# Softmax exponentials by quarter of the tokens, for all heads at once, with the maximum subtracted on VectorE first

## The chip, the cores and the metric

The kernel runs on one core of one Trainium2 chip. The metric is the device time of one execution in microseconds (us); lower is better. The granted clock is the share of TensorE's full clock that the chip allows it. Runs of a state called slow (a longer time at a lower granted clock) are left out of every ratio. The profile is one execution taken by the hardware profiler; its span runs from the first to the last instruction and is about 1.3 us shorter than the device time.

## The reference

One token for each of two batch entries goes through an adaLN-conditioned block: grouped-query attention over a cached context, then an MLP.

```python
B, Sq, D = (2, 1, 1024); Hq, Hkv, Sk, Dh = (32, 4, 32768, 128)   # B part: F = 3584
mod = (_silu(c) @ w_mod).reshape(c.shape[0], 6, 1, -1)
h = _layernorm(x) * (1 + ca) + sa
# attention, q from h @ wq; each K/V head serves 8 query heads
scores = jnp.einsum('bhqd,bhkd->bhqk', q, k) * Dh ** (-0.5)
p = _softmax(scores, axis=-1)
o = jnp.einsum('bhqk,bhkd->bhqd', p, v)
x = x + ga * (o @ wo)
h = _layernorm(x) * (1 + cb) + sb
x = x + gb * (_gelu(_layernorm(h) @ w1 + b1) @ w2 + b2)
```

All inputs are bf16. K and V together are 134.2 MB, the weights about 44 MB. Each byte is used once, so there is little arithmetic for each byte fetched.

## The kernel before

The eight pairs of batch entry and K/V head are eight rounds of a loop. A round fetches two halves of K (4 MB each) and one V (8 MB), each into one buffer that is reused in the next round. The sync engine issues the transfers in this order, and each waits until the previous user of its place is done:

```python
def add_k(i, hf):   # 2 x 16 KB in each partition
    add(("K", i, hf), [2, TPC * D], ..., hf * 32 * KB, f"K{hf}")
def add_v(i):       # NCH = 4 quarters x 16 KB in each partition
    add(("V", i), [NCH, TPC * D], ..., 64 * KB, "V")
...
for i in range(NBG):
    add_k(i, 0); add_k(i, 1); add_v(i)
# then wo, w1, w2 into the places that K, V and wq leave
```

In a round TensorE transposes K in groups of 8 tiles (`tr`), ScalarE and VectorE evict the transposes, and TensorE makes the scores from them (`qk`). Then come the softmax over 8 heads and the product with V (`pv`):

```python
def softmax_3():    # the maximum of each head, times -SCALE, on all partitions
    pe(... psM[:, 128:128 + HPG] ...)
    dve(lambda e: e.tensor_scalar(negm[:, :], psM[:, 128:128 + HPG], -SCALE, None, ALU.mult), ...)
def exp(h):         # one head, all 256 columns, row sum accumulated
    act(lambda e: e.activation(E_sb[:, :, h, :], S_sb[:, h, :]..., ACT.Exp, bias=negm[:, h:h + 1], scale=SCALE,
                               accum_out=rowsum[:, h:h + 1]), reads=ROW + ["negm"], writes=["E_sb", "rowsum"], ...)
def pv(i, cc):      # a quarter of the tokens: 16 matmuls with 512 columns
    ... reads=[it.reg, "E_sb"], writes=["psO"] ...
def row_sums():     # rowsum -> rsum16 (VectorE) -> sum over partitions (TensorE) -> reciprocal
    ...
for i in range(NBG):
    ...             # transposes and scores
    softmax_1(); softmax_2(); softmax_3()
    for h in range(HPG):
        exp(h)
    row_sums()
    for cc in range(NCH):
        pv(i, cc)
    extract(); extract_2(i)
```

An exponential of one head covers the tokens of all four quarters, so the first quarter of `pv` needs all eight of them. The program also puts the matmul of `row_sums` ahead of `pv`.

## Time and profile before

| what | before |
|---|---|
| device time, median | 420.11 us (3 runs, 420.03 to 420.19) |
| bytes read from HBM | 178.28 MB |
| busy: TensorE, VectorE, ScalarE | 281.7, 169.6, 167.9 us of 418.9 |
| end of the loop of eight rounds | 374.05 us |

These lines are from the page of the profile of the kernel before: the span, the busy tenths of the DMA engines in 40 equal slices, the bytes per second in those slices, the bytes in all, and the shares of the chain of work that ended last.

```profile
span 418.9 us, 11665 instructions
...
DMA  9989999999999999999999999999999999999995
GB/s 373 449 380 449 444 408 487 397 410 442 447 432 422 435 444 426 429 447 451 404 429 469 419 413 441 447 432 422 447 432 422 419 460 451 389 441 433 417 435 243
...
HBM read 178.28 MB, written 0.00 MB: 426 GB/s over the span
...
PE 56%; DMA 22%; ACT 8%; issue 7%; DVE 6%; SPq 0%; ACTq 0%
```

The DMA line shows 9, that is 90% or more, in every slice but the third, an 8, and the last, a 5. The last line gives 56% of the chain to TensorE. The chain follows what ran without a visible wait.

The view by windows: each line is one round, cut where its last matmul ends. After the window come its length, then busy us (and instructions) of PE, PEld, DVE, ACT and POOL, the granted TensorE clock, the share of the DMA engines' time and GB/s.

```profile
core 0: us, PE busy (x) PEld busy (x) DVE busy (x) ACT busy (x) POOL busy (x), PEclk, DMA share, GB/s
62.50:106.86 44.36, 32.89 (x585) 27.72 (x585) 18.70 (x34) 20.44 (x33) 0.00 (x0) 0.76 1.01 432
145.03:182.99 37.96, 28.32 (x585) 24.27 (x586) 19.16 (x36) 20.01 (x33) 0.44 (x2) 0.87 1.01 436
297.73:336.02 38.29, 28.65 (x585) 24.27 (x586) 19.16 (x36) 20.01 (x33) 0.44 (x2) 0.87 1.00 431
```

A round moves 16.78 MB, which takes 38.7 us at 433 GB/s. TensorE's rounds 2 to 8 take 37.7 to 39.3 us. The DMA engines have no idle time in any of them (share 1.00 or 1.01). What TensorE waits for in the whole kernel is in the view of the waits. A line names the engine, what it was about to write and the line of the kernel, then what it waited for; the numbers are us in total, times, longest:

```profile
PE psM L584 <- DVE rsum L583: 45.3, 8, 5.7
...
PE psM L596 <- DVE msum L591: 13.0, 8, 1.6
...
PE psKT L534 <- DMA K<-in_A_k_cache_dram: 4.6, 1, 4.6
```

It waits for the row sums ahead of PV in each round, for the sums of the masked output behind PV, and for a K transfer only once, in round 1. In the other rounds K has landed before it is wanted. The timeline of round 7 shows the first of these waits from inside (start, duration, engine, line, operation; in brackets the idle time just before):

```profile
321.97 0.17 DVE L563 TENSOR_SCALAR negm<-psM 128x8 f32<-128x8 f32 x1 [0.48 <-PE psM L562]
322.25 0.51 ACT L566 ACTIVATE E_sb<-S_sb,negm 128x256 bf16<-128x256 f32 x1 [2.71 <-DVE negm L563]
...
326.68 0.51 ACT L566 ACTIVATE E_sb<-S_sb,negm 128x256 bf16<-128x256 f32 x1
327.09 0.19 ACT L566 ACTIVATION_READ_ACCUMULATOR E_sb<-S_sb,negm 128x1 f32 x1
...
327.31 0.23 DVE L583 COPY rsum<-rowsum 128x128 f32<-128x128 f32 x1 [5.18 <-ACT E_sb L566]
...
327.59 0.59 PE L584 MATMUL psM<-onesf,rsum 128*128 128x1 f32 x2 [5.67 <-DVE rsum L583]
...
328.11 5.80 PE L576 MATMUL psZ<-V,E_sb 128*32 128x512 bf16 x64
```

Each exponential comes with a read of its accumulator (0.19 us), and the eight follow each other every 0.63 us. The maximum is ready at 322.14 us and the first PV matmul starts at 328.11. In those 6.0 us TensorE does one small matmul. This gap is what the change aims at.

### The profile page before, as it was taken

The page shows a single profiled execution, that of the slowest core. Times are in us where ns is not written, and L with a number is a line of the kernel's source. Part 1 is how long each engine was busy: PE and PEld are TensorE (multiplying, and loading weights), DVE is VectorE, ACT ScalarE, POOL GpSimd, SP SyncE. Part 2 cuts the span into 40 slices and gives each one's busy share as a digit, 9 for nine tenths or more (in the row PEclk, how much of TensorE's full clock was granted, in tenths as well). Part 3 has the DMA queues.
Part 4 walks back from the last instruction along what each step waited for, and adds up shares of the span by engine and source line. Part 5 has one row for each costly group of instructions (what it writes and reads, how often), then busy time and mean ns, then how long its engine had stood idle before and what let it go on. Part 6 is the DMA issues. An engine that isn't in the chain of part 4 may idle for free.

```text
span 418.9 us, 11665 instructions
## 1 busy us (share of the span) xinstructions
PE 281.7 (67%) x5183; PEld 223.5 (53%) x5183; DVE 169.6 (40%) x351; ACT 167.9 (40%) x275; POOL 6.8 (2%) x29
## 2 busy tenths in 40 slices
PE   1407539856892798389559928974895699274456
PEld 1104219852892498169529915972694299132314
DVE  1201106540772377157417724760574177220421
ACT  2000015544565166526545662645265356600100
POOL 3000000000000000000000000000000000000000
PEclk9976668965997799599869968995998699686565
DMA  9989999999999999999999999999999999999995
GB/s 373 449 380 449 444 408 487 397 410 442 447 432 422 435 444 426 429 447 451 404 429 469 419 413 441 447 432 422 447 432 422 419 460 451 389 441 433 417 435 243
DMA packets 5582, 178.43 MB, mean 426 GB/s; under 512 B 698, under 2 KB 706, under 8 KB 964
## 3 DMA queue, kind: packets, MB, share of 16 engines
q1 hardware_dynamic: 5572, 178.28, 98.7%
q8 instruction: 8, 0.13, 0.1%
q14 instruction: 2, 0.02, 0.0%
HBM read 178.28 MB, written 0.00 MB: 426 GB/s over the span
## 4 chain that ended last, share of the span: by engine, by line
PE 56%; DMA 22%; ACT 8%; issue 7%; DVE 6%; SPq 0%; ACTq 0%
PE psKT L534 28%; PE psZ L576 11%; DMA K<-in_A_k_cache_dram 10%; DMA w<-in_B_w_dram 9%; PE psS L546 6%; PE psZ L546 5%; ACT E_sb L566 4%; DMA wmod<-in_w_mod_dram 4%; DVE msum L591 2%; ACT KT_sb L538 2%; DVE m1c L551 1%; ACT S_sb L550 1%; PE psM L584 1%; PE psM L562 1%; PE psM L596 1%
## 5 line engine op out<-in xcount | busy, mean ns | idle before, releaser
L534 PE MATMUL psKT<-ident,K 128*128 128x128 bf16 x2048 | 154.5, 221 | 4.6 <-DMA K<-in_A_k_cache_dram 4.6
L538 ACT ACTIVATE KT_sb<-psKT 128x1024 bf16<-128x1024 bf16 x96 | 97.7, 1025 | 115.6 <-PE psKT L534 115.4
L540 DVE COPY KT_sb<-psKT 128x1024 bf16<-128x1024 bf16 x160 | 106.3, 689 | 44.3 <-PE psKT L534 43.5
L534 PEld LDWEIGHTS psKT<-ident,K 128*128 128x128 bf16 x2048 | 118.7, 98 | 5.8 <-DMA K<-in_A_k_cache_dram 4.7
L546 PE MATMUL psS<-qcur,KT_sb 128*128 128x8 bf16 x1024 | 44.3, 166 | 1.7 <-issue 1.7
L576 PE MATMUL psZ<-V,E_sb 128*32 128x512 bf16 x512 | 44.8, 527 | 0.0
L546 PE MATMUL psZ<-qcur,KT_sb 128*128 128x8 bf16 x1024 | 43.1, 167 | 0.8
L566 ACT ACTIVATE E_sb<-S_sb,negm 128x256 bf16<-128x256 f32 x64 | 32.5, 508 | 25.1 <-DVE negm L563 23.3
L546 PEld LDWEIGHTS psS<-qcur,KT_sb 128*128 128x128 bf16 x1024 | 39.2, 96 | 1.8 <-issue 1.8
L546 PEld LDWEIGHTS psZ<-qcur,KT_sb 128*128 128x128 bf16 x1024 | 37.9, 96 | 2.0 <-ACT KT_sb L538 1.4
L584 PE MATMUL psM<-onesf,rsum 128*128 128x1 f32 x16 | 4.7, 362 | 45.3 <-DVE rsum L583 45.3
L576 PEld LDWEIGHTS psZ<-V,E_sb 128*32 128x32 bf16 x512 | 16.7, 127 | 24.2 <-issue 20.0
L584 PEld LDWEIGHTS psM<-onesf,rsum 128*128 128x128 f32 x16 | 4.0, 311 | 46.1 <-DVE rsum L583 46.1
L589 DVE TENSOR_SCALAR msum<-psZ,mk 128x128 f32<-128x128 f32 x8 | 2.8, 351 | 43.1 <-PE psZ L576 43.1
L583 DVE COPY rsum<-rowsum 128x128 f32<-128x128 f32 x8 | 1.8, 227 | 41.4 <-ACT E_sb L566 41.4
L467 PE MATMUL psS<-wmod,inT 128*32 128x512 bf16 x32 | 4.8, 592 | 16.4 <-DMA wmod<-in_w_mod_dram 16.4
L551 DVE TENSOR_REDUCE m1c<-psZ 128x8 f32<-128x512 f32 x16 | 11.1, 693 | 10.2 <-ACT S_sb L550 10.1
L596 PE MATMUL psM<-msum,hmat 128*128 128x128 f32 x16 | 3.9, 326 | 13.0 <-DVE msum L591 13.0
L551 DVE TENSOR_REDUCE m1c<-psS 128x8 f32<-128x512 f32 x16 | 11.1, 693 | 3.2 <-ACT S_sb L550 3.1
L434 ACT ACTIVATE stat<-stat 128x2 f32<-128x2 f32 x3 | 0.6, 203 | 29.4 <-DVE stat L433 29.4
L557 PE MATMUL psM<-identf,m 128*8 128x128 f32 x16 | 3.4, 298 | 13.1 <-DVE m L554 13.1
L550 ACT ACTIVATE S_sb<-psZ 128x512 f32<-128x512 f32 x16 | 9.5, 595 | 6.1 <-PE psZ L546 6.1
(121 smaller groups left out, 172.7 us busy)
## 6 DMA issues: line engine op xcount, KB each, us to landing
K<-in_A_k_cache_dram SPq DMA_DIRECT2D x16, 4096.0 KB, 25.2
wq<-in_A_wq_dram SPq DMA_DIRECT2D x2, 4096.0 KB, 44.9
wo<-in_A_wo_dram SPq DMA_DIRECT2D x2, 4096.0 KB, 36.3
w<-in_B_w_dram SPq DMA_DIRECT2D x2, 3584.0 KB, 30.6
wmod<-in_w_mod_dram SPq DMA_DIRECT2D x1, 6144.0 KB, 30.0
w<-in_B_w_dram SPq DMA_DIRECT2D x3, 2048.0 KB, 35.7
wmod<-in_w_mod_dram SPq DMA_DIRECT2D x1, 4608.0 KB, 15.9
wmod<-in_w_mod_dram SPq DMA_DIRECT2D x1, 1536.0 KB, 6.2
```

What stands on the lines that cost most here:

```text
L467: pe(lambda e, w=it.view, k=k, kk=kk, ch=ch, n=n, q=q: e.matmul(bank[n][32 * q:32 * q + 32, :], lhsT=inT[:, k, :], rhs=w[:, kk, ch * 512:( ...
L534: pe(lambda e, kq=kq, jj=jj, w=kt, t=t: e.transpose(psKT[kq][:, jj * 128:(jj + 1) * 128], w[:, t, :], ident[:, :]), reads=[it.reg, "ident" ...
L538: act(lambda e, src=src: e.activation(KT_sb[g8][:, :, :], src, ACT.Copy), reads=[f"psKT{kq}"], writes=[f"KT_sb{g8}"], sem=f"ev{cc}_{g8}")
L540: dve(lambda e, src=src: e.tensor_copy(KT_sb[g8][:, :, :], src), reads=[f"psKT{kq}"], writes=[f"KT_sb{g8}"], sem=f"ev{cc}_{g8}")
L546: pe(lambda e, t=t, jj=jj: e.matmul(ps[:, t * HPG:(t + 1) * HPG], lhsT=KT_sb[g8][:, jj, :], rhs=qcur[:, :], start=True, stop=True), reads= ...
L550: act(lambda e: e.activation(Sc, ps.rearrange("p (t h) -> p h t", h=HPG), ACT.Copy), reads=[preg], writes=[f"S_sb_{cc}"], sem=f"sc{cc}")
L551: dve(lambda e: e.tensor_reduce(m1c[:, :, cc], ps.rearrange("p (t h) -> p h t", h=HPG), AX.X, ALU.max), reads=[preg], writes=[f"m1c{cc}"])
L566: act(lambda e: e.activation(E_sb[:, :, h, :], S_sb[:, h, :].rearrange("p (u t) -> p u t", t=4), ACT.Exp, bias=negm[:, h:h + 1], scale=SCA ...
L576: pe(lambda e, t4=t4, tg=tg, q=q: e.matmul(psO[32 * q:32 * q + 32, :], lhsT=E_sb[:, tg // 4, :, :].rearrange("p h t -> p (h t)"), rhs=vt[: ...
L584: pe(lambda e: e.matmul(psM[:, 144:145], lhsT=rsum16.rearrange("p g h e -> p (g h e)"), rhs=onesf[:, 0:1], start=True, stop=True), reads=[ ...
L591: dve(lambda e, q=q: e.scalar_tensor_tensor(out=msum[:, :], in0=psO[:, q * 128:(q + 1) * 128], scalar=mk4[:, q:q + 1], in1=msum[:, :], op0 ...
L596: pe(lambda e: e.matmul(psM[:, 256:384], lhsT=hmat.rearrange("p g h e -> p (g h e)"), rhs=msum[:, :], start=True, stop=True), reads=["hmat ...
```

## The change

The intent is to let PV start sooner. VectorE first subtracts each head's maximum from a quarter of the scores, for all 8 heads (512 columns), so one exponential without a bias can serve a quarter of all heads. PV of a quarter then waits for its own exponential only. Since a ScalarE instruction now mixes heads, the one sum in each partition that it accumulates (128x1 in the timeline above) would mix them too; VectorE sums each quarter instead, and the row-sum matmul moves behind PV. (`T.step` in the diffs only counts an engine's semaphore signals in a round; it follows the edits.)

```diff
--- before.py
+++ after.py
@@ -248,7 +248,7 @@
     out: bass.AP,
 ):
     T = Tracker(nc)
-    T.step["pe"], T.step["dve"], T.step["act"] = 72, 8, 7
+    T.step["pe"], T.step["dve"] = 72, 14
 
     def sb(name, shape, dtype=FP32):
         return nc.alloc_sbuf_tensor(name, list(shape), dtype)
@@ -303,12 +303,14 @@
     m1 = sb("m1", [128, HPG])
     gm = sb("gm", [HPG, 1])
     diag = sb("diag", [HPG, HPG])
-    negm = sb("negm", [128, HPG])
+    gmb = sb("gmb", [128, HPG])
     rowsum = sb("rowsum", [128, HPG])
+    rs4 = sb("rs4", [128, HPG, NCH])
     rinv = sb("rinv", [128, 1])
     S_sb = sb("S_sb", [128, HPG, NT])
     row = S_sb.rearrange("p h n -> p (h n)")
     ROW = [f"S_sb_{cc}" for cc in range(NCH)]
+    EREG = [f"E_sb_{cc}" for cc in range(NCH)]
     E_sb = sb("E_sb", [128, NT // 4, HPG, 4], BF16)
     qrow = E_sb.rearrange("p u h t -> p (u h t)")
     KT_sb = [sb(f"KT_sb{i}", [128, 8, 128], BF16) for i in range(NKT)]
@@ ... cut: the query projection uses E_sb as scratch and now names all four regions EREG @@
@@ -560,12 +562,18 @@
 
     def softmax_3():
         pe(lambda e: e.matmul(psM[:, 128:128 + HPG], lhsT=onesf[0:HPG, :], rhs=diag[:, :], start=True, stop=True), reads=["onesf", "diag"], writes=["psM"])
-        dve(lambda e: e.tensor_scalar(negm[:, :], psM[:, 128:128 + HPG], -SCALE, None, ALU.mult), reads=["psM"], writes=["negm"], sem="nm")
-
-    def exp(h):
-        act(lambda e: e.activation(E_sb[:, :, h, :], S_sb[:, h, :].rearrange("p (u t) -> p u t", t=4), ACT.Exp, bias=negm[:, h:h + 1], scale=SCALE,
-                                   accum_out=rowsum[:, h:h + 1]),
-            reads=ROW + ["negm"], writes=["E_sb", "rowsum"], sem="ex" if h == HPG - 1 else None)
+        dve(lambda e: e.tensor_copy(gmb[:, :], psM[:, 128:128 + HPG]), reads=["psM"], writes=["gmb"])
+
+    def exp(cc):
+        Sc = S_sb[:, :, cc * TPC:(cc + 1) * TPC]
+        Ec = E_sb[:, cc * TPC // 4:(cc + 1) * TPC // 4, :, :]
+        dve(lambda e: e.tensor_tensor(Sc, Sc, gmb[:, :].unsqueeze(2).to_broadcast([128, HPG, TPC]), ALU.subtract),
+            reads=[f"S_sb_{cc}", "gmb"], writes=[f"S_sb_{cc}"], sem=f"sb{cc}")
+        act(lambda e: e.activation(Ec, Sc.rearrange("p h (u t) -> p u h t", t=4), ACT.Exp, scale=SCALE), reads=[f"S_sb_{cc}"], writes=[f"E_sb_{cc}"], sem=f"ex{cc}")
+
+    def part_sum(cc):
+        Ec = E_sb[:, cc * TPC // 4:(cc + 1) * TPC // 4, :, :]
+        dve(lambda e: e.tensor_reduce(rs4[:, :, cc], Ec.rearrange("p u h t -> p h u t"), AX.XY, ALU.add), reads=[f"E_sb_{cc}"], writes=[f"rs4_{cc}"])
 
     def pv(i, cc):
         it = need("V", i)
@@ -577,9 +585,10 @@
                                                     rhs=vt[:, t4 * 512:(t4 + 1) * 512],
                                                     start=(cc == 0 and t4 < 4), stop=(cc == NCH - 1 and t4 >= TPC // 4 - 4),
                                                     skip_group_check=True),
-               reads=[it.reg, "E_sb"], writes=["psO"], mark=(t4 == TPC // 4 - 1))
+               reads=[it.reg, f"E_sb_{cc}"], writes=["psO"], mark=(t4 == TPC // 4 - 1))
 
     def row_sums():
+        dve(lambda e: e.tensor_reduce(rowsum[:, :], rs4[:, :, :], AX.X, ALU.add), reads=[f"rs4_{cc}" for cc in range(NCH)], writes=["rowsum"])
         dve(lambda e: e.tensor_copy(rsum16[:, :, :, :], rowsum[:, :].unsqueeze(1).unsqueeze(3).to_broadcast([128, 2, HPG, 8])), reads=["rowsum"], writes=["rsum16"], sem="rs")
         pe(lambda e: e.matmul(psM[:, 144:145], lhsT=rsum16.rearrange("p g h e -> p (g h e)"), rhs=onesf[:, 0:1], start=True, stop=True),
            reads=["onesf", "rsum16"], writes=["psM"])
@@ -623,11 +632,12 @@
         softmax_1()
         softmax_2()
         softmax_3()
-        for h in range(HPG):
-            exp(h)
+        for cc in range(NCH):
+            exp(cc)
+        for cc in range(NCH):
+            part_sum(cc)
+            pv(i, cc)
         row_sums()
-        for cc in range(NCH):
-            pv(i, cc)
         extract()
         extract_2(i)
         T.segments = None
```

More of the change, by code (lines that the diff above doesn't have):

```diff
@@ L507, in bass_adaLN_cond__gqa_block_cached__mixer_channel_mlp__decode_kernel @@
                reads=[it.reg, "inT"], writes=[breg[n]], mark=(ch % 4 == 3))
-    act(lambda e: e.activation(qrow[:, 0:512], bank[0][:, :], ACT.Copy), reads=[breg[0]], writes=["qrow0", "E_sb"])
-    dve(lambda e: e.tensor_copy(qrow[:, 512:1024], bank[1][:, :]), reads=[breg[1]], writes=["qrow1", "E_sb"])
+    act(lambda e: e.activation(qrow[:, 0:512], bank[0][:, :], ACT.Copy), reads=[breg[0]], writes=["qrow0"] + EREG)
+    dve(lambda e: e.tensor_copy(qrow[:, 512:1024], bank[1][:, :]), reads=[breg[1]], writes=["qrow1"] + EREG)
     for n in range(2):
@@ L513, in bass_adaLN_cond__gqa_block_cached__mixer_channel_mlp__decode_kernel @@
                                             lhsT=qrow[:, n * 512 + i * 128:n * 512 + (i + 1) * 128], rhs=idr, start=True, stop=True),
-               reads=[f"qrow{n}", "ident", "E_sb"], writes=["psM"], mark=(i == 3))
+               reads=[f"qrow{n}", "ident"] + EREG, writes=["psM"], mark=(i == 3))
     dve(lambda e: e.tensor_copy(qT[:, :, :], psM[:, 0:64].rearrange("p (b h) -> p b h", b=2)), reads=["psM"], writes=["qT"], sem="mo")
```

## The prediction

> **What bounds the kernel now.** The transfers. The page shows 178.28 MB read from HBM in a span of 418.9 us, DMA busy at 9 tenths in every slice, 98.7% of 16 engines' span in one queue. The view by windows, cut at the rounds of the attention loop, shows a DMA share of 0.99 to 1.01 and 430 to 437 GB/s in each of the eight. [...] About 2 us ahead of the first transfer and 5.5 us behind the last (final matmuls, output) are most of the rest.
>
> The chain of waits names TensorE (56%), but that chain only runs level with the transfers: its rounds are 37.7 to 39.3 us apart, and the 16.78 MB of a round take 38.7 us at 433 GB/s. TensorE waits for K once (4.6 us, round 1) and in rounds 2 to 8 never, because it runs some microseconds behind: the last K0 and V were issued at 307.4 and 334.0 us with medians of 25 and 28 us to landing, so they land near 333 and 362 us and are used at 336 and 367 us.
>
> **What the change removes.** By the timeline of one round, from the ready maximum (322.1) to PV's first matmul (328.1) TensorE idles 6.0 us: eight exponentials 0.63 us apart, the copy of row sums 0.23, their matmul 0.59.
>
> **What it adds.** Estimates from like instructions: a subtraction of 128x512 about 0.7 us (the f32 TENSOR_TENSOR takes 0.17 us at 16 columns, 0.29 at 128), an exponential of 128x512 0.6 to 0.7 (the ACT copy of that size 0.595), a partial sum 0.7 (the f32 reduction of 512 columns 0.693). PV can start 1.7 us after the maximum instead of 6.0. A quarter's PV takes 1.45 us, longer than subtraction or exponential, so later quarters don't wait. VectorE's subtractions and sums end near 5.9 us, before PV (7.5). Row-sum matmul and reciprocal move behind PV: 0.8 to 0.9 us back. Net: TensorE's chain gets about 3.4 us shorter per round, 27 us in all; VectorE gets 5 to 6 us more work per round.
>
> **How much is on the critical path.** Almost none. TensorE catches up with the transfers within two rounds and then waits for V and K, 3 to 4 us per round. Buffers free earlier, but the queue never runs empty now, so nothing ends earlier. Behind the loop, weights still take 39 us to arrive.
>
> **Predicted time:** 420.1 us, range 418.9 to 421.4. Chances: faster by over 2% 0.01, within 2% 0.97, slower 0.02.
>
> **What the profile would show.** Right: DMA share still 0.99 to 1.01 and 430 to 437 GB/s per round; rounds 38 to 39 us apart; new waits of TensorE for V before PV (2 to 3 us in most rounds) and for K at a round's start, 20 to 27 us in sum; the wait for row sums before PV (5.7 us per round) gone; the last PV near 362 to 364 us instead of 367; the same 5.5 us tail. Wrong: a DMA share under 0.95 in the loop, a round under 37 us, TensorE without waits for DMA, or subtractions far over 0.7 us with PV waiting for exponentials.
>
> **What would make it wrong.** A queue that was starved between transfers and that earlier issue fills (faster); [...] waits for V that delay its release until the queue empties.

The sum in the first paragraph came to about 417 us of the span of 418.9: the bytes at a rate that no trace of this case shows, and the 2 and 5.5 us around them. The term of the bytes is cut, so the "rest" is what it left of the span. At the 433 GB/s measured in a round the 178.28 MB take 411.7 us, with the 2 and 5.5 us about 419 (an estimate).

## The result

| | before | changed |
|---|---|---|
| device time, median of 6 runs | 420.16 us | 420.10 us |
| lowest to highest | 420.03 to 421.48 | 420.02 to 420.26 |
| end of the loop | 374.05 us | 371.32 us |
| start of the last round's PV | 366.6 us | 362.5 us |

The ratio is 0.9994 with a 95% interval of 0.9981 to 1.0007: the same time. A ratio here is the mean time of one kernel's fast runs over that of the other's fast runs of the same rounds, so it is not quite the ratio of the medians.

The page after the change (span, busy times, DMA tenths, bytes, the chain):

```profile
span 418.7 us, 11609 instructions
...
PE 291.0 (70%) x5183; PEld 231.3 (55%) x5183; DVE 209.6 (50%) x423; ACT 149.4 (36%) x179; POOL 6.8 (2%) x29
...
DMA  9989999999999999999999999999999999899995
...
HBM read 178.28 MB, written 0.00 MB: 426 GB/s over the span
...
DMA 71%; PE 24%; DVE 2%; issue 1%; ACT 1%; SPq 1%
```

VectorE's busy time rose from 169.6 to 209.6 us and TensorE's from 281.7 to 291.0, the bytes are the same, and the chain has turned over: 71% of it is now transfers, where it was 22%. The time did not move, though what the page names as the chain did.

The windows of the rounds after the change:

```profile
62.50:104.89 42.39, 33.00 (x584) 27.80 (x585) 23.65 (x43) 18.07 (x21) 0.00 (x0) 0.82 1.00 430
104.89:140.38 35.49, 29.83 (x585) 25.59 (x586) 24.17 (x45) 17.74 (x21) 0.44 (x2) 0.86 1.00 432
140.38:177.34 36.96, 28.85 (x585) 24.47 (x584) 24.09 (x45) 17.63 (x21) 0.44 (x2) 0.86 1.01 436
215.47:255.25 39.78, 31.00 (x584) 26.18 (x584) 24.17 (x45) 17.74 (x21) 0.44 (x2) 0.83 1.00 431
331.50:371.32 39.82, 30.99 (x585) 26.18 (x584) 24.16 (x45) 17.74 (x21) 0.44 (x2) 0.83 1.00 432
```

The DMA engines are as full as before and move the same 430 to 437 GB/s. Rounds 2 and 3 are short (35.5 and 37.0 us): there TensorE uses up the lead that the transfers had. From then on it can't be faster than they are. The waits show what it does instead:

```profile
PE psZ L584 <- DMA V<-in_A_v_cache_dram: 20.0, 6, 4.5
...
PE psM L605 <- DVE msum L600: 13.3, 8, 1.7
...
PE psKT L536 <- DMA K<-in_A_k_cache_dram: 11.5, 6, 4.6
...
PE psZ L584 <- ACT E_sb L572: 3.3, 2, 1.6
```

The wait for the row sums ahead of PV (45.3 us) is gone. In its place stand 20.0 us of waits for V and 11.5 us for K, of which 4.6 us were there before. The timeline of the last round:

```profile
359.81 2.50 DVE L570 TENSOR_TENSOR S_sb<-S_sb,gmb 128x512 f32<-128x512 f32 x4
360.54 2.44 ACT L572 ACTIVATE E_sb<-S_sb 128x512 bf16<-128x512 f32 x4 [3.77 <-DVE S_sb L570]
...
362.51 6.34 PE L584 MATMUL psZ<-V,E_sb 128*32 128x512 bf16 x64 [2.93 <-DMA V<-in_A_v_cache_dram]
...
368.78 0.38 PE L593 MATMUL psM<-onesf,rsum 128*128 128x1 f32 x2
...
369.20 0.17 DVE L595 RECIPROCAL rinv<-psM 128x1 f32<-128x1 f32 x1 [4.03 <-PE psM L593]
369.28 0.33 DVE L598 TENSOR_SCALAR msum<-psZ,mk 128x128 f32<-128x128 f32 x1
...
370.83 0.49 PE L605 MATMUL psM<-msum,hmat 128*128 128x128 f32 x2 [1.67 <-DVE msum L600]
```

The four subtractions start at 359.81 us and the first exponential at 360.54; it takes about 0.61 us, so it is done near 361.2. PV starts only at 362.51, when V has landed. The row-sum matmul stands behind PV and takes 0.38 us; the reciprocal after it overlaps the first step of the masked sum, which starts 0.08 us later.

### The profile page after: what moved, and what is told of

The parts are those of the page before. It is cut to its first block, busy times and chain, and to the rows that moved or that the text cites. A ratio compares the mean times of both kernels' runs of the same rounds, so it can differ in the third digit from the quotient of the medians.

```text
span 418.7 us, 11609 instructions
## 1 busy us (share of the span) xinstructions
PE 291.0 (70%) x5183; PEld 231.3 (55%) x5183; DVE 209.6 (50%) x423; ACT 149.4 (36%) x179; POOL 6.8 (2%) x29
## 3 DMA queue, kind: packets, MB, share of 16 engines
q1 hardware_dynamic: 5572, 178.28, 98.8%
HBM read 178.28 MB, written 0.00 MB: 426 GB/s over the span
## 4 chain that ended last, share of the span: by engine, by line
DMA 71%; PE 24%; DVE 2%; issue 1%; ACT 1%; SPq 1%
DMA V<-in_A_v_cache_dram 39%; DMA wo<-in_A_wo_dram 10%; DMA K<-in_A_k_cache_dram 10%; PE psZ L584 10%; DMA w<-in_B_w_dram 9%; PE psKT L536 8%; DMA wmod<-in_w_mod_dram 4%; PE psS L548 1%; PE psZ L548 1%; PE psS L655 1%; PE psZ L729 1%; PE psZ L469 1%; ACT KT_sb L540 0%; PE psS L469 0%; DVE m1c L553 0%
## 5 line engine op out<-in xcount | busy, mean ns | idle before, releaser
L536 PE MATMUL psKT<-ident,K 128*128 128x128 bf16 x2048 | 163.1, 229 | 11.5 <-DMA K<-in_A_k_cache_dram 11.5
L536 PEld LDWEIGHTS psKT<-ident,K 128*128 128x128 bf16 x2048 | 126.7, 102 | 13.0 <-DMA K<-in_A_k_cache_dram 12.7
L584 PE MATMUL psZ<-V,E_sb 128*32 128x512 bf16 x512 | 46.4, 541 | 23.2 <-DMA V<-in_A_v_cache_dram 20.0
L584 PEld LDWEIGHTS psZ<-V,E_sb 128*32 128x32 bf16 x512 | 18.7, 130 | 47.7 <-issue 38.8
L572 ACT ACTIVATE E_sb<-S_sb 128x512 bf16<-128x512 f32 x32 | 19.5, 630 | 29.6 <-DVE S_sb L570 29.6
L570 DVE TENSOR_TENSOR S_sb<-S_sb,gmb 128x512 f32<-128x512 f32 x32 | 20.0, 685 | 0.3
L576 DVE TENSOR_REDUCE rs<-E_sb 128x8 f32<-128x512 bf16 x32 | 19.7, 675 | 0.0
L553 DVE TENSOR_REDUCE m1c<-psZ 128x8 f32<-128x512 f32 x16 | 11.1, 693 | 10.2 <-ACT S_sb L552 10.1
L595 DVE RECIPROCAL rinv<-psM 128x1 f32<-128x1 f32 x8 | 1.3, 168 | 27.7 <-PE psM L593 27.7
L559 PE MATMUL psM<-identf,m 128*8 128x128 f32 x16 | 4.3, 369 | 13.1 <-DVE m L556 13.1
L469 PEld LDWEIGHTS psS<-wmod,inT 128*32 128x32 bf16 x32 | 1.1, 132 | 19.3 <-DMA wmod<-in_w_mod_dram 18.0
```

The costliest lines, as they stand in the source:

```text
L469: pe(lambda e, w=it.view, k=k, kk=kk, ch=ch, n=n, q=q: e.matmul(bank[n][32 * q:32 * q + 32, :], lhsT=inT[:, k, :], rhs=w[:, kk, ch * 512:( ...
L536: pe(lambda e, kq=kq, jj=jj, w=kt, t=t: e.transpose(psKT[kq][:, jj * 128:(jj + 1) * 128], w[:, t, :], ident[:, :]), reads=[it.reg, "ident" ...
L553: dve(lambda e: e.tensor_reduce(m1c[:, :, cc], ps.rearrange("p (t h) -> p h t", h=HPG), AX.X, ALU.max), reads=[preg], writes=[f"m1c{cc}"])
L559: pe(lambda e: e.matmul(psM[0:HPG, 0:128], lhsT=m1[:, :], rhs=identf[:, :], start=True, stop=True), reads=["m1", "identf"], writes=["psM"])
L570: dve(lambda e: e.tensor_tensor(Sc, Sc, gmb[:, :].unsqueeze(2).to_broadcast([128, HPG, TPC]), ALU.subtract), reads=[f"S_sb_{cc}", "gmb"], ...
L572: act(lambda e: e.activation(Ec, Sc.rearrange("p h (u t) -> p u h t", t=4), ACT.Exp, scale=SCALE), reads=[f"S_sb_{cc}"], writes=[f"E_sb_{c ...
```

## The experiments

There were eight runs, all with a profile, each timed beside the kernel before on the same chip. Four of them halve the V transfers, so that the transfers no longer bound the loop and TensorE's chain comes into view. Their V data is wrong on purpose (their outputs still passed the comparison with the reference, whose tolerance doesn't see it).

### Half of V, kernel before

```diff
-    add(("V", i), [NCH, TPC * D], A_v_cache[...].rearrange(...), 64 * KB, "V")
+    add(("V", i), [NCH // 2, TPC * D], A_v_cache[...].rearrange(...)[:, 0:NCH // 2, :], 64 * KB, "V")
-    vt = it.view[:, cc, :]
+    vt = it.view[:, cc % 2, :]
```

> The kernel before, but each V transfer brings only the first half of V and quarters 2 and 3 of PV read quarters 0 and 1 again (result wrong on purpose). All engine work stays, the bytes fall by 33.6 MB to 144.7 MB. Theory (transfers bound the kernel before, TensorE's chain runs level with them): TensorE's rounds stay near 38.0 us, the loop still ends near 374 us, behind it 11 MB of weights are left to fetch, so about 404 us; DMA share in the loop falls to about 0.75. Rival 1 (the kernel before is bound by TensorE's chain, whatever the transfers do): same span of the loop, but then the changed kernel should have been faster, so the pair with the next run decides. Rival 2 (transfers alone set the time): 420 - 77 = 343 us.

Measured: 407.95 us (median of 4, 405.02 to 410.26), ratio to the kernel before 0.9691. The loop ended at 373.73 us against 374.05 with all of V. One round in the windows, and the wait ahead of PV:

```profile
182.70:220.43 37.73, 28.10 (x586) 24.23 (x586) 19.14 (x36) 20.00 (x33) 0.44 (x2) 0.86 0.82 334
```

```profile
PE psM L584 <- DVE rsum L583: 45.3, 8, 5.7
```

With a quarter fewer bytes a round, the rounds kept their length (37.73 us here, 37.75 with all of V) and the DMA share fell to 0.78 to 0.82 in rounds 2 to 7 (0.75 expected). So the kernel before is at a balance: in the loop TensorE's chain is as long as the transfers. All that the missing bytes saved came behind the loop, where fewer bytes were left. There the estimate was 4 us too low (404 against 407.95): the last 6 us of this run hold no transfers at all, so the MLP's own chain of matmuls ended last, which the estimate had not counted.

### Half of V, changed kernel

The same edit on the changed kernel.

> The changed kernel with the same halved V (result wrong on purpose). Theory (the change shortens TensorE's chain by about 3.4 us a round, hidden at full bytes by waits for V and K): rounds near 34.7 us, no waits for V, 27 us less than the halved kernel before, about 377 us. Rival (the change saves nothing on the chain, or gives it back through the extra 5 us of VectorE work per round or a lower TensorE clock): within 5 us of the halved kernel before.

Measured: 375.84 us (median of 5, 374.06 to 377.52). The mean is 375.70 us against 407.80 of the halved kernel before, a ratio of 0.921.

```profile
206.65:240.68 34.03, 28.36 (x585) 24.12 (x586) 24.10 (x45) 17.63 (x21) 0.44 (x2) 0.90 0.91 370
```

```profile
PE psM L605 <- DVE msum L600: 13.3, 8, 1.7
PE psZ L584 <- ACT E_sb L572: 13.2, 8, 1.6
```

This is the test of the mechanism: with the transfers out of the way, the same change is worth 32 us. The loop ends at 342.96 instead of 373.73 us, that is 30.8 us in eight rounds or 3.85 us a round. TensorE's busy time within the loop is nearly the same in both (232.3 and 232.8 us by the windows), so the difference is idle time: 45.3 us of waits ahead of PV became 13.2 us, for the exponentials, which is 32.1 us. The 40 us of additional VectorE work did not get in the way. The rival, that the change saves nothing on the chain, falls.

### Half of V, changed kernel, PV waits for all exponentials

```diff
-               reads=[it.reg, f"E_sb_{cc}"], writes=["psO"], ...
+               reads=[it.reg] + EREG, writes=["psO"], ...
```

> The changed kernel with halved V, and PV of every quarter waits for all four exponentials. It parts the two halves of the change: fewer, larger exponentials against the overlap of PV with them. Theory: PV starts after 4 exponentials of 0.61 us instead of one, 1.8 us later, so 15 us more than the halved changed kernel (about 392 us), still 12 us less than the halved kernel before. Rival (all the gain is the overlap): level with the halved kernel before. Rival (all is the merging of instructions): level with the halved changed kernel.

Measured: 401.32 us (median of 4, 399.14 to 402.66).

```profile
PE psZ L584 <- ACT E_sb L572: 27.6, 8, 3.5
```

```profile
217.83:255.60 37.77, 30.30 (x586) 25.70 (x585) 24.18 (x45) 17.74 (x21) 0.45 (x2) 0.82 0.82 333
255.60:292.41 36.81, 29.35 (x586) 24.38 (x586) 24.13 (x45) 17.63 (x21) 0.44 (x2) 0.86 0.84 342
```

The waits ahead of PV are 27.6 us against 13.2, so the overlap of PV with the exponentials is worth 14.4 us of waiting, as expected (15). The other 17.7 us of the 32.1 come with the rest of the change: four larger exponentials in place of eight, and the row sums behind PV. The time missed its expectation (401.3 us against 392): the loop became 25.3 us longer than in the halved changed kernel. The rest is in TensorE's busy time in the loop, 243.3 us against 232.8 for the same instructions. The two rounds shown differ in the same way: at a granted clock of 0.82 the busy time is 30.30 us, at 0.86 it is 29.35.

These means hide where the clock is low. Cut into windows of 0.25 us, the loops show a granted clock of 1.00 or 0.50, with values between only where it changes. In every softmax gap a stretch at 0.50 begins, which lasts 10.2 us in rounds 2 to 8 here and 6.8 to 7.0 us in the halved changed kernel. Five of these rounds here (one there) also begin with some 3.3 us at 0.50: the 32 transposes from 217.79 us took 3.46 us, where the first 32 of round 7 of the kernel before took 1.92. In all TensorE had half the clock for about 107 us of this loop and for 68 us of the other. In the round that begins at 217.83 us, PV started at 247.40 us and the clock rose about 4.3 us later. No run here sets the clock alone, so what lowers and raises it, and why the stretches are longer in this variant, is left open. All four of its runs have a lower mean clock (0.80 to 0.83) than all five of the halved changed kernel (0.84 to 0.86). So 25 us is what giving up the overlap costs here, and 14.4 us of it is the waiting that the overlap hides.

### Half of V, kernel before, row sums behind PV

```diff
-        row_sums()
         for cc in range(NCH):
             pv(i, cc)
+        row_sums()
```

> The kernel before with halved V and only one part of the change: the row-sum matmul and the reciprocal moved behind PV. Theory: PV starts 0.8 us earlier and ends with 0.8 to 0.9 us more behind it, so within 2 us of the halved kernel before. Rival (taking the row sums out of PV's way is a real part of the gain): 6 us less.

Measured: 402.66 us (median of 4, 401.80 to 406.01), 4.5 us less in the mean than the halved kernel before. That is nearer to the rival than to the theory, but with four runs each, which scatter by 4 to 5 us, the difference is uncertain by some 3.5 us, and the times decide for neither.

```profile
PE psZ L576 <- ACT E_sb L566: 43.2, 8, 5.4
```

The wait ahead of PV went from 45.3 to 43.2 us, 2.1 us less in all eight rounds. The other 3.6 us of the loop's 5.6 us are TensorE's busy time (232.3 to 228.6 us), where shorter row-sum matmuls (4.7 to 3.1 us in all) and the granted clock mix. Most of the loop's gain (3.3 us) is in rounds 1 and 6, in which the halved kernel before had a clock of 0.77 and 0.83: there its stretch at half clock lasted 13.8 us, here 10.2. The rounds at 0.86 in both differ by only 0.1 to 0.3 us. So the move of the row sums is a small part of the 32 us (2.1 us of the waits); how small in time can't be told from this run.

### Full bytes, half of the transposes

```diff
-                tr(i, cc, g8)
+                if g8 % 2 == 0:
+                    tr(i, cc, g8)
-        kq = g8 % NPKT
+        kq = (g8 // 2) % NPKT
-   ... lhsT=KT_sb[g8][:, jj, :], rhs=qcur[:, :] ...
+   ... lhsT=KT_sb[g8 - g8 % 2][:, jj, :], rhs=qcur[:, :] ...
-    T.step["pe"], T.step["dve"] = 72, 14
+    T.step["pe"], T.step["dve"] = 56, 14
```

> The changed kernel at full bytes, with every second group of 8 K transposes and its eviction left out and the scores taken from the group before it (result wrong on purpose): about 9 to 10 us less TensorE work a round, and K buffers free earlier. Theory (the transfers are a floor and the queue is never empty): 420 us, within 0.5%; waits for V and K grow by 60 us or more in sum. Rival (earlier release of buffers starts transfers earlier and that is worth time): 410 us or less.

Measured: 419.97 us (419.91 to 420.49), ratio 0.9998 (0.9983 to 1.0013).

```profile
PE psZ L584 <- DMA V<-in_A_v_cache_dram: 54.3, 8, 7.7
PE psKT L536 <- DMA K<-in_A_k_cache_dram: 19.5, 16, 4.6
```

Half of the transposes are gone, which is 18% of TensorE's busy time in the loop (242.8 to 199.8 us). K buffers are free earlier (in round 7 the next K transfers are issued 8 us after the round begins, in the changed kernel 13 us), and the time is the same. The transfers are a floor. The waits for V and K grew by 42.3 us, from 31.5 to 73.8, which is the 43 us by which TensorE's busy time fell. I had expected 60 us or more, because I had counted the transposes' own durations in full. By line these fell by 67 us (163.1 to 96.1), but they overlap with the score matmuls, and TensorE also spent more of the loop at half clock (about 171 us against 101). In the changed kernel eight transposes took 1.01 us at half clock (from 298.35 us) and 0.61 at the full one (from 221.55 us).

### Full bytes, kernel before, five exponentials more

```diff
+        for h in range(5):
+            exp(h)
         for h in range(HPG):
             exp(h)
-    ... T.step["act"] = 72, 8, 7
+    ... T.step["act"] = 72, 8, 12
```

> The kernel before at full bytes with five of its eight exponentials run twice: TensorE's chain longer by 5 x 0.63 = 3.2 us a round, 25 us in all, the opposite of the change (result unchanged). Theory (the kernel before sits near the balance point: its rounds of 38.0 us are as long as a round's transfer of 38.7): now TensorE's chain bounds, rounds near 41.3 us, the loop ends near 399 us instead of 374, and after the last V is released 11 MB of weights and the tail take 30 us: about 430 us, and the DMA share in the loop falls to 0.94. Rival (softmax is off the critical path with slack to spare, so either direction is free): 420 us. Rival (all of it counts): 445 us.

Measured: 435.33 us (432.82 to 438.56), ratio 1.0367 (1.0316 to 1.0417).

```profile
PE psM L584 <- DVE rsum L583: 70.7, 8, 8.8
```

```profile
233.34:274.38 41.04, 28.24 (x586) 24.26 (x586) 19.15 (x36) 23.01 (x43) 0.45 (x2) 0.83 0.97 409
```

The wait ahead of PV grew by 25.4 us, as intended. The loop ended at 397.33 us (expected 399), but the total was 5 us over the estimate. With the chain at 41 us a round, the single K and V buffers are released later and the transfers run with gaps: the DMA share is 0.96 to 0.98 and the rate 407 to 418 GB/s in rounds 2 to 8, about 411 on average where the kernel before has 434. Over those 287.8 us that is 15 us of lost transfer time (an estimate from the two rates), as much as the whole difference. The share of 0.97 alone would be about 9 us of it; why the rate fell by more than the share is not shown. So the kernel before had no room: the next 3 us a round cost 15 us.

### Full bytes, changed kernel, five exponentials more

```diff
+        for _ in range(5 if cc == 0 else 0):
+            act(lambda e: e.activation(Ec, ..., ACT.Exp, scale=SCALE), reads=[f"S_sb_{cc}"], writes=[f"E_sb_{cc}"])
         act(lambda e: e.activation(Ec, ..., ACT.Exp, scale=SCALE), ..., sem=f"ex{cc}")
-    T.step["pe"], T.step["dve"] = 72, 14
+    T.step["pe"], T.step["dve"], T.step["act"] = 72, 14, 5
```

> The changed kernel at full bytes with its first quarter's exponential run six times instead of once: TensorE's chain longer by 5 x 0.61 = 3.1 us a round, 24 us in all, nearly the load that cost the kernel before 15 us (result unchanged). Theory (the change turned the 3.9 us a round that it takes off the chain into slack against the transfers): the chain of 34.05 us becomes 37.1, still shorter than the 38.5 us of a round's transfers, so about 420 us, and the 27 us of waits for V and K shrink to 10 us or less. Rival (the changed kernel has no slack, the waits for V and K have another cause): 430 us or more.

Measured: 420.12 us (420.08 to 421.47), ratio 1.0011 (0.9991 to 1.0030). One run of the kernel before was slow (435.11 us at a clock of 0.694) and is left out; another, at 424.66 us, counts.

```profile
PE psZ L586 <- ACT E_sb L574: 39.6, 8, 5.0
...
PE psKT L536 <- DMA K<-in_A_k_cache_dram: 7.4, 3, 4.6
```

The wait ahead of PV is now 39.6 us for the exponentials, no wait is put down to V, and 2.8 us of waits for K are left beyond round 1. Nearly the same load that cost the kernel before 15 us costs the changed kernel nothing. The change made slack, and this run spends it.

### Full bytes, changed kernel, the last weight in finer pieces

```diff
-W2_ITEMS = (..., (16, 24, 128), (24, 27, 144), (27, 28, 150))
+W2_ITEMS = (..., (16, 20, 128), (20, 24, 136), (24, 27, 144), (27, 28, 150))
```

> The changed kernel with one transfer of the last weight (8 rows of w2, 2 MB) split in two of 1 MB, so that TensorE starts the final matmuls on the first half while the rest arrives (result unchanged). Theory (what is left besides the bytes is the tail behind the last transfer): the first 32 of the 96 final matmuls run about 2.4 us earlier, the last ones start as soon as the last bytes land; 0.8 to 1.2 us less than 420.1, so about 419.1 us. Rival (the last transfers land together, whatever their split): 420.1 us.

Measured: 419.96 us (419.92 to 420.11), ratio to the kernel before 0.9994 (0.9981 to 1.0008). The changed kernel has 0.9994 as well. The final matmuls, first in the changed kernel and then with the split:

```profile
413.27 2.91 PE L729 MATMUL psZ<-gT,w 128*128 128x2 bf16 x96 [0.30 <-DMA w<-in_B_w_dram]
```

```profile
412.91 1.84 PE L729 MATMUL psZ<-gT,w 128*128 128x2 bf16 x64
...
415.26 1.01 PE L729 MATMUL psZ<-gT,w 128*128 128x2 bf16 x32 [0.51 <-DMA w<-in_B_w_dram]
```

The expectation failed. Sixty-four of the 96 matmuls do start earlier, but by 0.36 us (412.91 against 413.27) and not by 2.4, and the last 32 wait until 415.26 us for the last transfer. In the changed kernel the 96 ran back to back and ended at 416.2, in step with the landings already. No version was found that beats both kernels.

## Why the prediction was right

The time (420.1 predicted, 420.10 measured) and the mechanism were right. The time alone says little of the mechanism: where the transfers are a floor, any saving on TensorE's chain gives 420 us. How much the change saves on the chain was tested with half of V only. Point by point:

- **Transfers bound the kernel, the chain of waits only runs level with them.** The floor is shown: leaving out 18% of TensorE's busy time in the loop changes nothing (419.97 us). That the two run level in the kernel before is shown too: with half of V its rounds keep their length while the DMA share falls to 0.78 to 0.82, so there TensorE's chain alone is as long, and easing either one alone gains little in the loop (it ends 0.3 us sooner with fewer bytes, 2.7 us sooner with the shorter chain). All eight rounds of both kernels lie at 430 to 437 GB/s, and at 430 to 438 with half of the transposes; that no higher rate is possible was not shown.
- **PV can start 1.7 us after the maximum.** In the second round, in which PV did not wait for V, the maximum is ready at 131.29 us and PV's first matmul at 132.72, so 1.4 us. The subtraction took 0.685 us in the mean (predicted 0.7), the exponential 0.630 (0.6 to 0.7), the partial sum 0.675 (0.7).
- **Row sums behind PV give 0.8 to 0.9 us back.** This term was mis-sized. The matmul takes 0.38 us there, against 0.59 ahead of PV, and the reciprocal overlaps what follows it, so the wait behind PV grew only from 1.62 to 1.66 us a round: about 0.4 us given back. With PV's start 1.4 us after the maximum, these two terms would make the saving 4.2 us a round (6.0 - 1.4 - 0.4, an estimate); with half of V the chain got shorter by 3.85 us, not 3.4. Changes of the clock from round to round are in that mean.
- **TensorE then waits for V and K, 20 to 27 us in sum.** It was 20.0 us for V and 6.9 us more for K, 26.9 in all. The waits for V were six of 3.3 us on average, longest 4.5, where 2 to 3 had been predicted.
- **Signs to look for.** DMA share, rate, the vanished wait, PV of the last round at 362.5 us and the tail of 5.4 us came as said. The sign "a round under 37 us means wrong" was badly drawn: rounds 2 and 3 were 35.5 and 36.96 us, because TensorE caught up with the transfers in them, as the same text had said it would. Later rounds reached 39.8 us, beyond the 38 to 39 predicted.
- **Not foreseen:** TensorE's busy time rose by 9.3 us for the same matmuls, nearly all in the transposes (154.5 to 163.1 us), with a granted clock of 0.82 to 0.83 in four of the last five rounds, where before it was mostly 0.86 to 0.87. Windows of 0.25 us show where: rounds 2, 5, 6, 7 and 8 begin with 3.2 to 6.8 us at half clock, which the kernel before has in none of its rounds 2 to 8. The waits absorbed it.

## What to carry to other kernels

Compare the length of a round of the busiest engine with the bytes of a round over the measured rate; where they are level, the chain that the profile names can belong to an engine whose speed-up is worth nothing. Here such a speed-up turned into waits for transfers, whose sum was predicted, and its worth showed only when the bytes fell or the engine got other work: 32 us and 15 us, from a change that measured zero. When two variants of an experiment are compared, take the waits and the busy times apart before the difference is given a cause, because busy times here moved by some 4% (243.3 against 232.8 us) for the same instructions.
